# A gated-recurrence layer with two feed-forward layers: wider blocks from the second chunk, the low part of four pairs by TensorE, and other places for the wide operands

## The chip, the cores and the metric

The kernel runs on one core of a Trainium2 chip. The time is the device time of one execution in microseconds (us). Three executions of the kernel before took 1081.52 to 1082.71 us, with a median of 1082.33 us.

## The reference

Two parts follow each other.

```python
# 1. recurrence: B=4 batches, H=8 heads, S=768 steps, D=48
mag = sqrt(a_re**2 + a_im**2); scale = min(mag, 0.999) / (mag + 1e-6)
for t in range(S):
    S_re, S_im = ar*S_re - ai*S_im, ar*S_im + ai*S_re      # state of D x D per head
    S_re += outer(k[t], v[t])
    y[t] = q[t] @ S_re
# 2. two layers over all 3072 tokens x 384, d_ff = 2048
h = x @ w_in;  g = max(h, 0) + alpha * min(h, 0);            x = g @ w_out
h = x @ w_in2; g = h if h >= 1, 0 if h <= -1, else (h+1)**2/4;  out = g @ w_out2
```

The weights come as 64-bit floats. The result has to be close to single precision, so each product of the two layers is made of three matmuls: high part times high part, high times low, low times high.

## The kernel before

**Tokens.** The sequence is cut into 6 chunks of 128 steps. A pair is half a chunk (two batches, 256 tokens); there are 12 pairs, 0 to 11. A pair is made in two slabs of 128 tokens, called p.r (pair 3 has slabs 3.0 and 3.1). VectorE (DVE) makes the products of the gates (`levels`, `fixup`, tile `C`) and multiplies them with q and k (`qkh`, line 265). Twelve DMAs of the queue SP then gather one slab into the tile `st`, of which there is one buffer (lines 269 and 272). TensorE (PE) works on it in `slab_matmul`: scores `sp` (line 286), transposes `kp` (295), outputs `yp` (309) and the state's update `dp` (318). The tokens' high part goes from `yp` to the buffer `xbuf` by ScalarE (ACT, line 312), and the low part, `yp` minus the high part, by DVE (line 313).

**Layers.** `moe` takes a block of tokens through the 16 column groups of a layer. For group f, `h_mm` does 9 matmuls h (line 396), `evac` turns h into a high part `gh` and a low part `gl` with ACT and DVE (lines 409 to 425), and two groups later `y_mm` does 9 matmuls acc (line 436). A block is named by its layer and its first pair (1_2 begins with pair 2) or its number in layer 2 (2_0 to 2_5). Before, blocks 1_0 to 1_3 have one pair, so that a matmul streams 256 columns, and 1_4, 1_6, 1_8 and 1_10 two pairs, 512 columns, as all of layer 2. h1_4.5 is below the h of block 1_4 and group 5, a1_4.5 its acc.

**Weights.** Each of the 16 groups of a layer has one buffer. The raw 64-bit words land there, DVE decodes them (lines 343 to 349), and the high and low part take the same buffer. Weights of layer 2 can take it only after the acc of block 1_10 that reads the old ones. Before, the first four groups (`AHEAD = 4`) use other buffers, `wearly` and `rawearly`, and are decoded before that.

**Order.** A list scheduler sets the order on every engine at build time, by its own estimate of times. On the chip each engine and the queue SP work through their lists in order. Evacuations and the stores of results have priority in it. Which slabs stand in the program ahead of a block is set by `LOOK`: all pairs up to two beyond the block's own.

**Addresses.** In bytes within a partition, modulo 512, the operands of the 512-column matmuls begin here (from the addresses of the built programs; weights and rows within a tile are multiples of 512 apart):

| operand | before | after |
|---|---|---|
| weights `w` of both layers | 480 | 480 |
| weights `wearly`, two tiles | 160 and 256 | none |
| tokens in buffer 0 of `xbuf` (1_4, 1_8, 2_0, 2_2, 2_4) | 32 | 480 |
| tokens in buffer 1 of `xbuf` (1_6, 1_10, 2_1, 2_3, 2_5; after also 1_2) | 480 | 480 |
| `gh` and `gl` | 480 | 224 |

Of the kernel before, what the change touches and what calls it, by code (L numbers as in the profile page):

```python
# [22 lines left out]
GI = 4
NG = T // GI
NU = T // 16
NK = 3
NJ = 2 * NK
NR = 4 * NK
NFC = 16
BLOCKS_A = [1] * 4 + [2] * 4  # L30
HALF_UNTIL, LOOK = 6, 2
VH = 64
VW = H * VH + 32
F64_LEAST = float(np.array(0x38000000, np.uint32).view(np.float32))
F64_MOST = float(np.array(0x47EFFFFF, np.uint32).view(np.float32))
PRIO = 100000
TS = 8
E0, E1, E2, SIDE = 6, 1, 2, 4
AHEAD = 4
PIN = True  # L40
BY_PE = 0
LAG, GB = 2, 3
SCRATCH = 512
RAWS = 11
SHIFT = 8
MI_MOST = 1e4
CAP = 1e10
# [9 lines left out]
def tile_kernel(ctx: ExitStack, tc, ri, qk, v, w1, w2, alpha, seq, vseq, out):  # L57
    nc = tc.nc
    const = ctx.enter_context(tc.tile_pool(name="const", bufs=1))
# [6 lines left out]
    ps_at = ctx.enter_context(tc.tile_pool(name="ps_at", bufs=2, space=PSUM))  # L66
    V, A, G = nc.vector, nc.scalar, nc.gpsimd
# [4 lines left out]
    nident = const.tile([128, 128], F32R, name="nident")  # L72
# [14 lines left out]
        G.memset(t, 0.0)  # L87
        states.append(t)
    chk = const.tile([128, NC, 2, NR], F32, name="chk")
    fac = const.tile([128, NJ, NG + 1], F32, name="fac")  # L90
    def xview(n, wide):

        o = SHIFT if wide == (n == 0) else 0
        return xbuf[n][:, o:o + 2 * NK * 512].rearrange("p (l k n) -> p l k n", l=2, k=NK)

    xbuf, wfirst = {}, const.tile([128, 4, 2 * DM], F32, tag="x1", name="wfirst")
# [14 lines left out]

    x2d = dram.tile([128, NK, NT], F32, name="x2d")
# [102 lines left out]
    def levels(c, js):  # L215
        nj = js.stop - js.start
        C, mie = Cs[c][:, :, js], mis[c][:, js]
        if c == 0:
            V.memset(C[:, 0, :, 0], 1.0)
            V.memset(C[:, 1, :, 0], 0.0)  # L220
        else:
            A.activation(C[:, :, :, 0], Cs[c - 1][:, :, js, NG], AF.Copy)

        def place(i):
            return C[:, :, :, 1 + NG * (GI - 1 - i):1 + NG * (GI - i)]

# [48 lines left out]
    def slab_matmul(p, r, xt, col):  # L275
        c, h2 = divmod(p, 2)
        vt, sn = vts.pop((p, r)), states[2 * h2 + r]

        def slot(h, m):
            return 6 * (h % 2) + 3 * m + h // 2 if h < 6 else 12 + 2 * (h - 6) + m  # L280

        am, kps = [], []
        for f in range(2):
            sp = ps_at.tile([T, 4, T], F32, tag="at", name=f"sp{p}_{r}_{f}")
            for h in range(4):
                nc.tensor.matmul(sp[:, h], st[0:96, slot(4 * f + h, 1)], st[0:96, slot(4 * f + h, 0)], start=True, stop=True)  # L286
            a = p2.tile([T, 4, T], F32, tag="am", name=f"am{p}_{r}_{f}")
            V.tensor_tensor(a, sp, mask.unsqueeze(1).to_broadcast([T, 4, T]), op=ALU.mult)  # L288
            am.append(a)
            yield  # L290
        if c < NC - 1:
            for f in range(2):
                kp = ps_at.tile([T, 4, 96], F32, tag="at", name=f"kp{p}_{r}_{f}")
                for h in range(4):
                    nc.tensor.transpose(kp[:, h], st[0:96, slot(4 * f + h, 1)], ident[0:96, 0:96])
                kt = p2.tile([T, 4, 96], F32, tag="kt", name=f"kt{p}_{r}_{f}")
                A.activation(kt, kp, AF.Copy)
                kps.append(kt)
                yield

        yp = ps_at.tile([128, NK, T], F32, tag="at", name=f"yp{p}_{r}")
        parts = [(j, q, 4 * j + q, 0) for j in range(2) for q in range(4)]
        parts += [(2, q, 2 * q + o, 32) for o in range(2) for q in range(4)]
        sides = [lambda h, w: (sn[:, w:w + 32], st[:, slot(h, 0)])] if c > 0 else []
        sides.append(lambda h, w: (vt[:, w:w + 32], am[h // 4][:, h % 4]))
        for n, side in enumerate(sides):
            for k, (j, q, h, o) in enumerate(parts):
                lhs, rhs = side(h, VH * h + o)
                nc.tensor.matmul(yp[32 * q:32 * q + 32, j], lhs, rhs, start=(n == 0 and k < 4),  # L309
                                 stop=(n + 1 == len(sides) and k >= len(parts) - 4))  # L310
            yield
        A.activation(xt[:, 0, :, col:col + T], yp, AF.Copy)
        V.tensor_tensor(xt[:, 1, :, col:col + T], yp, xt[:, 0, :, col:col + T].bitcast(F32), op=ALU.subtract)
        yield
        if kps:
            dp = ps_at.tile([96, H, VH], F32, tag="at", name=f"dp{p}_{r}")
            for h in range(H):
                nc.tensor.matmul(dp[:, h], kps[h // 4][:, h % 4], vt[:, VH * h:VH * h + VH], start=True, stop=True)  # L318
            dst = sn[0:96].rearrange("p (h d) -> p h d", d=VH)
            if c == 0:  # L320
                A.activation(dst, dp, AF.Copy)
            else:
                V.tensor_tensor(dst, dp, dst, op=ALU.add)
            yield
# [470 lines left out]
def _layout(q, k, v, a_re, a_im, moe_w_in, moe_w_out, moe_alpha, moe2_w_in, moe2_w_out):  # L795
# [12 lines left out]
    vh = vp[..., :H * VH].reshape(NPAIR, 2, T, H, VH)
    vh[..., 0:32] = vs[..., 0:32]
    for o in range(2):  # L810
        vh[..., o::2, 32 + 16 * o:48 + 16 * o] = vs[..., o::2, 32:48]
    vp[..., :H * VH] = vh.reshape(NPAIR, 2, T, H * VH)
# [10 lines left out]
    al = np.ascontiguousarray(moe_alpha.reshape(NFC, 128).T)  # L823
# [29 lines left out]
```

## Time and profile before

| | us |
|---|---|
| median of three executions | 1082.33 |
| the profiled execution, its whole time | 1085.48 |
| its span, first to last instruction | 1083.7 |
| busy in the span: PE, DVE, ACT, POOL | 992.6, 860.7, 464.9, 49.8 |

The profile is of one execution. It lists engines, queues and waits. PE is busy 92% of the span. The clock of PE that the profile shows as granted is 1.00 (2.4 GHz) from 340.4 us to 1081.1 us without a break, and falls to 0.50 (1.2 GHz) in several stretches before. Block 1_1 is on PE from 177 us, 1_2 from 217 us, 1_3 from 274 us, 1_4 from 342 us, 1_6 from 437 us, 1_8 from 527 us, 1_10 from 609 us, and the blocks of layer 2 begin at 674, 741, 807, 874, 940 and 1006 us. In a row of instructions the start is counted from the span's start, "x9" says that nine followed each other, and the last part in brackets is the idle time before them and what ended it.

### The profile page before, as it was taken

To read this page: it belongs to the slowest core of one execution; us is meant where nothing else is said; L and a number is where in the kernel's file an instruction comes from. 1 tells how busy PE (TensorE), PEld (TensorE's weight loads), DVE (VectorE), ACT (ScalarE), POOL (GpSimd) and SP (SyncE) were. 2 spreads that over 40 slices of the span, in tenths; PEclk is the share of its full clock that TensorE was granted. 3 is DMA by queue.
4 is the path that set the end of the run, shared out by engine and by line. 5 is a ranking of instruction groups with operands and counts; after the bars stand their busy time and mean duration, and the time that the engine had idled before them with its cause. 6 is when DMAs were issued, how large, how long until landed. Compare 5 with 4: busy or idle time off the path is not lost.

```text
span 1083.7 us, 16959 instructions
## 1 busy us (share of the span) xinstructions
PE 992.6 (92%) x6401; PEld 837.1 (77%) x6401; DVE 860.7 (79%) x1750; ACT 464.9 (43%) x784; POOL 49.8 (5%) x108
## 2 busy tenths in 40 slices
PE   1369779999987999999999999999999999999997
PEld 0248668989986788888788888788888888888885
DVE  6889979989998999999995769976978855545553
ACT  3347455435633533643433546544444332332332
POOL 2020200000010010000000000000000000000000
PEclk9569888999998999999999999999999999999999
DMA  9570243062215214402332525403415110000000
GB/s 341 177 240 12 64 118 99 12 162 80 67 51 144 86 39 129 122 27 69 87 93 59 175 88 204 147 1 116 151 46 183 58 59 1 1 30 1 30 1 32
DMA packets 66504, 97.52 MB, mean 90 GB/s; under 512 B 8048, under 2 KB 37232, under 8 KB 66416
## 3 DMA queue, kind: packets, MB, share of 16 engines
q1 hardware_dynamic: 66416, 96.38, 28.9%
q8 instruction: 52, 0.85, 0.3%
q14 instruction: 36, 0.29, 0.1%
HBM read 68.03 MB, written 9.44 MB: 71 GB/s over the span
## 4 chain that ended last, share of the span: by engine, by line
PE 68%; DVE 17%; DMA 7%; SPq 3%; issue 2%; ACT 1%; DVEq 0%; ACTq 0%
PE acc L436 31%; PE h L396 30%; PE sp L286 3%; DMA st<-qkh 2%; PE yp L309 2%; SPq L272 2%; DVE t L410 2%; DVE qkh L265 1%; DVE gl L418 1%; DMA C<-in_ri 1%; PE dp L318 1%; DVE C L155 1%; DMA k<-in_qk 1%; DVE C L164 1%; DVE C L163 1%
## 5 line engine op out<-in xcount | busy, mean ns | idle before, releaser
L396 PE MATMUL h<-xbuf,w 128*128 128x512 f32 (+1 forms) x1800 | 395.8, 358 | 3.9 <-DVE t L410 1.3
L436 PE MATMUL acc<-gh,w 128*128 128x512 f32 (+1 forms) x1200 | 357.1, 361 | 3.3 <-ACT o L444 1.7
L396 PEld LDWEIGHTS h<-xbuf,w 128*128 128x128 f32 x1800 | 301.2, 188 | 54.0 <-DVE t L410 1.7
L436 PEld LDWEIGHTS acc<-gh,w 128*128 128x128 f32 x1200 | 217.4, 190 | 37.7 <-ACT o L444 2.4
L436 PE MATMUL acc<-gl,w 128*128 128x512 f32 (+1 forms) x600 | 212.7, 361 | 1.4 <-DVE gl L418 1.3
L422 DVE TENSOR_TENSOR m<-h,t 128x512 f32<-128x512 f32 x96 | 66.0, 689 | 79.7 <-ACT t L420 79.6
L436 PEld LDWEIGHTS acc<-gl,w 128*128 128x128 f32 x600 | 113.9, 190 | 18.6 <-DVE gl L418 2.0
L409 ACT ACTIVATE t<-h,sg 128x256 f32<-128x256 f32 (+1 forms) x128 | 74.0, 579 | 104.6 <-PE h L396 86.5
L424 ACT ACTIVATE gh<-t 128x512 fp32r<-128x512 f32 x96 | 60.5, 630 | 101.1 <-DVE t L423 92.1
L420 ACT ACTIVATE t<-h 128x512 f32<-128x512 f32 x96 | 57.3, 597 | 102.3 <-PE h L396 86.1
L425 DVE TENSOR_TENSOR gl<-t,gh 128x512 fp32r<-128x512 f32 x96 | 66.1, 689 | 43.8 <-ACT gh L424 43.7
L286 PE MATMUL sp<-st 96*128 96x128 f32 x384 | 69.4, 315 | 33.6 <-DMA st<-qkh 31.1
L411 ACT ACTIVATE gh<-t 128x256 fp32r<-128x256 f32 (+1 forms) x128 | 66.7, 522 | 70.9 <-DVE t L410 61.0
L286 PEld LDWEIGHTS sp<-st 96*128 96x128 f32 x384 | 63.1, 222 | 42.3 <-issue 29.7
L410 DVE SCALAR_TENSOR_TENSOR t<-h,sal,t 128x256 f32<-128x256 f32 (+1 forms) x128 | 78.1, 611 | 20.9 <-ACT t L409 20.7
L418 DVE TENSOR_TENSOR gl<-t,gh 128x256 fp32r<-128x256 f32 (+1 forms) x128 | 70.3, 550 | 4.5 <-ACT gh L411 4.4
L423 DVE SCALAR_TENSOR_TENSOR t<-t,m 128x512 f32<-128x512 f32 x96 | 66.1, 689 | 2.2
L379 PE MATMUL wd<-wfirst,ident 128*128 128x384 f32 x64 | 33.1, 620 | 36.0 <-DVE wfirst L349 35.6
L396 PE MATMUL h<-xbuf,wearly 128*128 128x512 f32 x216 | 54.2, 394 | 0.0
L288 DVE TENSOR_TENSOR am<-sp,mask 128x512 f32<-128x512 f32 x48 | 32.9, 684 | 21.4 <-PE sp L286 21.4
L436 PE MATMUL acc<-gh,wearly 128*128 128x512 f32 x144 | 49.1, 394 | 0.0
L396 PEld LDWEIGHTS h<-xbuf,wearly 128*128 128x128 f32 x216 | 40.5, 188 | 9.4 <-issue 0.2
(512 smaller groups left out, 1164.6 us busy)
## 6 DMA issues: line engine op xcount, KB each, us to landing
raw<-in_w SPq DMA_DIRECT2D x56, 384.0 KB, 6.1
st<-qkh SPq DMA_DIRECT2D x96, 144.0 KB, 3.2
rawc<-in_w SPq DMA_DIRECT2D x32, 384.0 KB, 3.5
C<-in_ri SPq DMA_DIRECT2D x10, 768.0 KB, 7.4
v<-in_v SPq DMA_DIRECT2D x24, 272.0 KB, 2.9
k<-in_qk SPq DMA_DIRECT2D x12, 384.0 KB, 5.7
q<-in_qk SPq DMA_DIRECT2D x12, 384.0 KB, 3.2
x2r<-x2d SPq DMA_DIRECT2D x6, 768.0 KB, 4.8
```

The lines of the kernel that those rows point to most:

```text
L286: nc.tensor.matmul(sp[:, h], st[0:96, slot(4 * f + h, 1)], st[0:96, slot(4 * f + h, 0)], start=True, stop=True)
L396: nc.tensor.matmul(hp[:, :n], wt[:, ws], xt[:, kk, :n], start=(k == 0), stop=(k == 8))
L409: A.activation(t, hp, AF.Copy, scale=sg[:, fc:fc + 1])
L410: V.scalar_tensor_tensor(t, hp, sal[:, fc:fc + 1], t, op0=ALU.mult, op1=ALU.max)
L411: A.activation(gh, t, AF.Copy)
L418: V.tensor_tensor(gl, t, gh.bitcast(F32), op=ALU.subtract)
L420: A.activation(t, hp, AF.Relu, scale=0.5, bias=0.5)
L422: V.tensor_tensor(m, hp, t, op=ALU.max)
L423: V.scalar_tensor_tensor(t, t, 1.0, m, op0=ALU.min, op1=ALU.mult)
L424: A.activation(gh, t, AF.Copy)
L425: V.tensor_tensor(gl, t, gh.bitcast(F32), op=ALU.subtract)
L436: nc.tensor.matmul(blk["acc"][m][:, :n], wt[:, ws], gt, start=(fc == 0 and q == 0), stop=(fc == NFC - 1 and q == 2))
```

## The change

1. `BLOCKS_A`: two blocks of one pair (1_0, 1_1), then five of two (1_2, 1_4, 1_6, 1_8, 1_10).
2. `XL_BY_PE = 4`: for pairs 0 to 3 the low part of the tokens is made by a PE matmul that adds minus the high part to `yp`, and an ACT copy, in place of DVE's subtraction.
3. `AHEAD = 0`: no `wearly`; all layer-2 weights are decoded into their own buffers, 14 groups in block 1_10 and two in 2_0.
4. The product with the carry (`tc`) is left out for chunk 0, where the carry is 1.
5. A head's values lie in 48 of 64 places, those of odd heads with the last 16 first; the states' update is 48 wide per head and not 64, and the load of v 512 wide and not 544.
6. Some small tiles are allocated before `xbuf`, and the wide blocks use the other offset (`SHIFT`) of each buffer.

```diff
-BLOCKS_A = [1] * 4 + [2] * 4
+BLOCKS_A = [1] * 2 + [2] * 5
-VW = H * VH + 32
+VW = H * VH
-AHEAD = 4
+AHEAD = 0
+XL_BY_PE = 4
...
+    wchk = const.tile([128, 2, NFC], F32, name="wchk")
+    al = const.tile([128, NFC], F32, name="al")
+    sg = const.tile([128, NFC], F32, name="sg")
     def xview(n, wide):
-        o = SHIFT if wide == (n == 0) else 0
+        o = SHIFT if wide == (n == 1) else 0
...
-        yield from cmul(f"tc{nm}_", C[:, :, :, 4], lambda n: C[:, n:n + 1, :, 0], (nj,))
+        if c:
+            yield from cmul(f"tc{nm}_", C[:, :, :, 4], lambda n: C[:, n:n + 1, :, 0], (nj,))
...
-        parts = [(j, q, 4 * j + q, 0) for j in range(2) for q in range(4)]
-        parts += [(2, q, 2 * q + o, 32) for o in range(2) for q in range(4)]
+        parts = [(j, q, 4 * j + q, q % 2 * 16) for j in range(2) for q in range(4)]
+        parts += [(2, q, 2 * q + o, 32 - 48 * o) for o in range(2) for q in range(4)]
...
-        V.tensor_tensor(xt[:, 1, :, col:col + T], yp, xt[:, 0, :, col:col + T].bitcast(F32), op=ALU.subtract)
+        if p < XL_BY_PE:
+            nc.tensor.matmul(yp, nident, xt[:, 0, :, col:col + T], start=False, stop=True, skip_group_check=True)
+            A.activation(xt[:, 1, :, col:col + T], yp, AF.Copy)
+        else:
+            V.tensor_tensor(xt[:, 1, :, col:col + T], yp, xt[:, 0, :, col:col + T].bitcast(F32), op=ALU.subtract)
...
-            dp = ps_at.tile([96, H, VH], F32, tag="at", name=f"dp{p}_{r}")
+            dp = ps_at.tile([96, H, D], F32, tag="at", name=f"dp{p}_{r}")
-                nc.tensor.matmul(dp[:, h], kps[h // 4][:, h % 4], vt[:, VH * h:VH * h + VH], start=True, stop=True)
+                nc.tensor.matmul(dp[:, h], kps[h // 4][:, h % 4], vt[:, VH * h:VH * h + D], start=True, stop=True)
```

The scheduler makes a new order of it. On PE the scores of slab 3.1 (`sp3_1`) stand before in the middle of block 1_2, whose tokens are then pair 2 alone:

```order
L396 MATMUL h1_2_6_2814<-xbuf1_1346,w1_6_700 128x256 x8
L286 MATMUL sp3_1_0_1844<-st_91 128x128
L286 MATMUL sp3_1_1_1851<-st_91 128x128
L396 MATMUL h1_2_6_2814<-xbuf1_1346,w1_6_700 128x256
L436 MATMUL acc1_2_0_2724<-gh1_2_4_2773,w1_4_602 128x256
```

After, slab 3.1 stands between the last acc of block 1_1 and the first h of block 1_2, which now has both pairs:

```order
L443 MATMUL acc1_1_2_2007<-gh1_1_15_2340,w1_15_1303 128x256
L288 MATMUL sp3_1_0_1841<-st_91 128x128
L288 MATMUL sp3_1_1_1848<-st_91 128x128
L288 MATMUL sp3_1_0_1841<-st_91 128x128 x3
...
L325 MATMUL dp3_1_1906<-v3_1_1821,kt3_1_1_1867 96x48 x4
L317 MATMUL yp3_1_1870<-xbuf1_1340,nident_84 128x384
L403 MATMUL h1_2_0_2937<-xbuf1_1340,w1_0_202 128x512
L403 MATMUL h1_2_1_2963<-xbuf1_1340,w1_1_265 128x512
```

PE has no layer matmul left between block 1_1 and the tokens of slab 3.1. In the queue SP the gather of slab 5.1 stands before behind one of the two loads of chunk 4 (`C4`):

```order
L139 DMA q6_3280<-in_qk 128x768
L129 DMA C4_4084<-in_ri 128x12x128
L269 DMA st_91<-qkh5_1_3264 48x768 x4
L272 DMA st_91<-qkh5_1_3264 32x2x128
L272 DMA st_91<-qkh5_1_3264 16x2x128 x2
```

After, it stands behind both loads and that of `k8`:

```order
L140 DMA q6_2850<-in_qk 128x768
L130 DMA C4_3654<-in_ri 128x12x128 x2
L135 DMA k8_3658<-in_qk 128x768
L271 DMA st_91<-qkh5_1_2834 48x768 x4
L274 DMA st_91<-qkh5_1_2834 32x2x128
```

Two loads, 1.1 MB, have moved ahead of the gather; for slab 3.1 both orders have this form. On DVE the first decode step of layer-2 weights in block 1_10 (`wsecond<-raw2_4`) comes before after the evacuation of group 6:

```order
L418 TENSOR_TENSOR gl1_10_6_6921<-t1_10_6_6919,gh1_10_6_6920 128x512
...
L343 TENSOR_SCALAR wsecond_6269<-wsecond_6269 128x768
...
L345 TENSOR_SCALAR wsecond_6269<-wsecond_6269 128x768
L348 SCALAR_TENSOR_TENSOR wsecond_6269<-raw2_4_6935,wsecond_6269 128x768
```

After, it is that of weight group 0, and it comes after the first evacuation step of group 4:

```order
L417 SCALAR_TENSOR_TENSOR t1_10_4_6413<-h1_10_4_6403,sal_112,t1_10_4_6413 128x512
L350 TENSOR_SCALAR wsecond_6357<-wsecond_6357 128x768
L425 TENSOR_TENSOR gl1_10_4_6415<-t1_10_4_6413,gh1_10_4_6414 128x512
L352 TENSOR_SCALAR wsecond_6357<-wsecond_6357 128x768
L355 SCALAR_TENSOR_TENSOR wsecond_6357<-raw2_0_6354,wsecond_6357 128x768
```

From there to the `gl` of group 2 of block 2_0, DVE has 99 instructions where it had 79 before.

## Rows read from the trace of the kernel before

**Rows 1.** Stages: us; busy of PE, PEld, DVE, ACT, POOL (instructions), PEclk, DMA

```profile
217.00:342.00 125.00, 114.02 (x1231) 109.92 (x1229) 113.27 (x306) 52.69 (x111) 7.40 (x22) 0.95 0.38 101
342.00:609.00 267.00, 261.01 (x2003) 216.50 (x2002) 241.52 (x546) 113.14 (x180) 13.92 (x36) 1.00 0.30 83
609.00:720.00 111.00, 110.09 (x482) 90.02 (x481) 96.51 (x140) 61.99 (x91) 0.00 (x0) 1.00 0.39 133
720.00:1075.00 355.00, 355.00 (x1550) 290.53 (x1549) 220.12 (x316) 129.58 (x205) 0.00 (x0) 1.00 0.15 52
330.20:340.40 10.20, 8.91 (x88) 7.82 (x88) 6.61 (x25) 1.27 (x4) 1.58 (x6) 0.50 0.57 166
```

**Rows 2.** Timeline of PE, slab 5.1: start, length, line, what

```profile
331.33 3.55 PE L286 MATMUL sp<-st 96*128 96x128 f32 x14 [5.41 <-DMA st<-qkh]
...
337.03 1.93 PE L309 MATMUL yp<-st,state 128*32 128x128 f32 x32
...
342.14 0.97 PE L396 MATMUL h<-xbuf,w 128*128 128x512 f32 x3
```

**Rows 3.** Timeline of DVE, the k product of slab 3.1

```profile
226.38 0.95 DVE L265 TENSOR_TENSOR qkh<-C,k 128x768 f32<-128x768 f32 x1
```

**Rows 4.** Timeline of SP's queue, around the gathers of slabs 3.1 and 5.1

```profile
228.98 1.25 SPq L129 DMA_DIRECT2D C<-in_ri  x2
...
313.44 5.13 SPq L272 DMA_DIRECT2D st<-qkh  x8
...
322.58 0.39 SPq L129 DMA_DIRECT2D C<-in_ri  x1
...
326.21 7.54 SPq L272 DMA_DIRECT2D st<-qkh  x8
```

**Rows 5.** Timeline of PE, slab 3.1, then the first h of 1_6 and 1_8

```profile
240.38 0.68 PE L286 MATMUL sp<-st 96*128 96x128 f32 x4 [2.36 <-DVE C L161]
...
251.58 1.08 PE L309 MATMUL yp<-st,state 128*32 128x128 f32 x32
...
436.82 0.94 PE L396 MATMUL h<-xbuf,w 128*128 128x512 f32 x3
...
527.43 0.94 PE L396 MATMUL h<-xbuf,w 128*128 128x512 f32 x3
```

**Rows 6.** The chain of waits: start, length, what (blocks 1_4, 1_10 and 2_2)

```profile
393.21 2.09 PE acc L436 x9
...
635.19 2.04 PE acc L436 x9
...
871.88 2.09 PE acc L436 x9
```

**Rows 7.** DVE by line and shape: count | busy us, mean ns | idle before

```profile
L410 DVE SCALAR_TENSOR_TENSOR t<-h,sal,t 128x512 f32<-128x512 f32 x64 | 47.6, 744 | 17.1 <-ACT t L409 17.0
L418 DVE TENSOR_TENSOR gl<-t,gh 128x512 fp32r<-128x512 f32 x64 | 43.8, 684 | 4.2 <-ACT gh L411 4.2
L410 DVE SCALAR_TENSOR_TENSOR t<-h,sal,t 128x256 f32<-128x256 f32 x64 | 30.4, 477 | 3.8 <-ACT t L409 3.7
L418 DVE TENSOR_TENSOR gl<-t,gh 128x256 fp32r<-128x256 f32 x64 | 26.5, 417 | 0.3 <-ACT gh L411 0.2
L313 DVE TENSOR_TENSOR xbuf<-yp,xbuf 128x384 fp32r<-128x384 f32 x24 | 13.2, 549 | 1.3 <-ACT xbuf L312 1.3
L383 DVE TENSOR_TENSOR w<-wsecond,w 128x768 fp32r<-128x768 f32 x12 | 11.4, 949 | 1.1 <-ACT w L374 1.1
L348 DVE SCALAR_TENSOR_TENSOR wsecond<-raw,wsecond 128x768 int32<-128x768 int32 x12 | 11.4, 948 | 0.0
L343 DVE TENSOR_SCALAR wsecond<-wsecond 128x768 f32<-128x768 f32 x16 | 8.8, 553 | 7.7 <-ACT wsecond L342 7.7
```

**Rows 8.** Timeline of DVE in blocks 1_10 and 2_0

```profile
642.32 0.56 DVE L343 TENSOR_SCALAR wsecond<-wsecond 128x768 f32<-128x768 f32 x1 [1.48 <-ACT wsecond L342]
...
697.89 0.68 DVE L425 TENSOR_TENSOR gl<-t,gh 128x512 fp32r<-128x512 f32 x1
```

**Rows 9.** Timeline of PE, the last acc of a1_10.0 and of a1_10.4

```profile
624.83 0.84 PE L436 MATMUL acc<-gh,w 128*128 128x512 f32 x3
...
636.84 0.39 PE L436 MATMUL acc<-gh,w 128*128 128x512 f32 x1
```

More of the change, by code (lines that the diff above doesn't have):

```diff
@@ L89, in tile_kernel @@
     chk = const.tile([128, NC, 2, NR], F32, name="chk")
-    fac = const.tile([128, NJ, NG + 1], F32, name="fac")
+    wchk = const.tile([128, 2, NFC], F32, name="wchk")
+    al = const.tile([128, NFC], F32, name="al")
+    sg = const.tile([128, NFC], F32, name="sg")
     def xview(n, wide):
-        o = SHIFT if wide == (n == 0) else 0
+        o = SHIFT if wide == (n == 1) else 0
         return xbuf[n][:, o:o + 2 * NK * 512].rearrange("p (l k n) -> p l k n", l=2, k=NK)
@@ L101, in tile_kernel @@
     alloc_x(0)
-    wchk = const.tile([128, 2, NFC], F32, name="wchk")
+    fac = const.tile([128, NJ, NG + 1], F32, name="fac")
     V.memset(fac, ABOVE)
@@ L107, in tile_kernel @@
     V.memset(cap[:, :, 0], 1.0)
-    al = const.tile([128, NFC], F32, name="al")
-    sg = const.tile([128, NFC], F32, name="sg")
     sal = const.tile([128, NFC], F32, name="sal")
@@ L312, in slab_matmul @@
         A.activation(xt[:, 0, :, col:col + T], yp, AF.Copy)
-        V.tensor_tensor(xt[:, 1, :, col:col + T], yp, xt[:, 0, :, col:col + T].bitcast(F32), op=ALU.subtract)
+        if p < XL_BY_PE:
[3 more added lines that the diff above has]
+            V.tensor_tensor(xt[:, 1, :, col:col + T], yp, xt[:, 0, :, col:col + T].bitcast(F32), op=ALU.subtract)
         yield
         if kps:
-            dp = ps_at.tile([96, H, VH], F32, tag="at", name=f"dp{p}_{r}")
+            dp = ps_at.tile([96, H, D], F32, tag="at", name=f"dp{p}_{r}")
             for h in range(H):
-                nc.tensor.matmul(dp[:, h], kps[h // 4][:, h % 4], vt[:, VH * h:VH * h + VH], start=True, stop=True)
-            dst = sn[0:96].rearrange("p (h d) -> p h d", d=VH)
+                nc.tensor.matmul(dp[:, h], kps[h // 4][:, h % 4], vt[:, VH * h:VH * h + D], start=True, stop=True)
+            dst = sn[0:96].rearrange("p (h d) -> p h d", d=VH)[:, :, 0:D]
             if c == 0:
@@ L807, in _layout @@
     vp = np.zeros((NPAIR, 2, T, VW), dtype=v.dtype)
[L808 to L812, printed above, removed]
+    vh = vp.reshape(NPAIR, 2, T, H, VH)
+    vh[..., 0::2, 0:D] = vs[..., 0::2, :]
+    vh[..., 1::2, 0:16], vh[..., 1::2, 16:D] = vs[..., 1::2, 32:], vs[..., 1::2, 0:32]
     def pack_w(wi, wo):
```

## The prediction

> **What bounds the kernel now.** I read the busy time by stages first [rows 1]. From 342 us on PE is nearly always busy: 261.0 of 267 us, 110.1 of 111, 355.0 of 355. There only fewer or quicker matmuls, or a lost wait, change the time. In the last stretch 1550 matmuls take 355.0 us, 229.0 ns each. From 217 to 342 us PE is busy 114.0 of 125 us and DVE 113.3: neither is the bound alone, so I read who waits for whom. The timeline of PE at slab 5.1 shows that it had waited 5.41 us for the gather into `st`, that its matmuls from there ran slowly (the granted clock is 0.50 in that stretch, the lower of the two levels [rows 1]), and that block 1_4 began at 342.14 [rows 2]. I take that moment as the mark of the early part: what comes before it counts by how early it lets 1_4 start.
>
> The timeline of DVE gives the end of the k product of slab 3.1, 226.38 + 0.95 = 227.3 us [rows 3]. In SP's queue two loads of `C` stand between it and the gather [rows 4], and the scores of that slab follow at 240.38 [rows 5]. The starts of 1_6 and 1_8 in the same view give the length of a wide block, 436.82 to 527.43, 90.6 us [rows 5]. Then the chain of waits, which lists matmuls by nines: the same nine take 2.04 us in block 1_10 and 2.09 in 1_4 and 2_2 [rows 6]. The first stand at 480 modulo 512 with all their operands (buffer 1), the others have tokens at 32 (buffer 0). Last, DVE by shapes [rows 7], and the decode of layer-2 weights around 1_10 and 2_0 [rows 8, 9].
>
> **Early part: wide 1_2.** Block 1_2 was pair 2 alone and now holds pairs 2 and 3, so it can't start before slab 3.1 is done. Ahead of that slab's k product DVE loses 6 subtractions of 0.549 us, 3.3, and 4 + 4 evacuation steps of 0.477 and 0.417 us, which belonged to 1_2, 3.6 [rows 7]. The eight steps of `tc`, under 1 us together by my estimate, I leave against the 0.08 us by which one DVE instruction begins before the other ends (227.25 against 227.33 [rows 3]). DVE has little idle time there, so the product ends 7 us earlier, at 220.3. From it to the scores it was 240.38 − 227.33 = 13.05 us; the queue's order around that gather is unchanged, so the scores come at 233.4. PE will then have been without layer work for some ten microseconds, and I expect the lower clock, as at slab 5.1, where scores to first h took 342.14 − 331.33 = 10.8 us and `yp` 1.93 us against 1.08 at full clock [rows 2, 5]. First h of 1_2: 233.4 + 10.8 = 244.2.
>
> Its length: 288 matmuls, 32 nines at 2.04 us, are 65.3 us. 1_6 took 90.6, with four slabs in it: (90.6 − 65.3)/4 = 6.3 us a slab. 1_2 holds three (4.0, 4.1, 5.0): 65.3 + 19.0 = 84.3. It ends at 328.5. Slab 5.1 comes next. Its gather is now queued behind both loads of `C` and one of k, where one `C` load was behind it [rows 4]. These loads wait for nothing late: the gather of slab 5.0 is gone from the queue by 319, and I take the new one as landed before 328.5, since DVE has 6.9 us less to do. So PE goes on at the higher clock: 9 to 10.8 us, the lower end being the 10.8 less the 0.85 us of `yp` and about as much for the rest. Then 1_4 begins at 337.5 to 339.3, against 342.14: −2.8 to −4.6, **−4 taken**. The bounds are far apart. If the scores are as early as the product allows and the clock stays up, 1_2 starts at 238 and 1_4 at 331.3, −11; if the gather is late by what DVE gives back, it is +9 (worked out with the rivals). The value taken stands nearest to the measured steps, 13.05 and 10.8.
>
> `XL_BY_PE` exchanges 8 subtractions of 0.549 us for 8 matmuls of 384 columns and 8 copies by ACT. Seven of the eight chains lie in PE's idle time or beside 1_1. At slab 3.1 the chain is `yp`, copy, matmul, copy in place of `yp`, copy, subtraction: 0 to +0.6 us. It is inside the bounds above. Values 48 wide: 0 for PE, in whose slabs weight loads are as many as before; 0 for DMA. The wide evacuation of pairs 2 and 3 saves DVE 16 × (2 × (0.477 + 0.417) − 0.744 − 0.684) = 5.8 us [rows 7], hidden behind PE inside 1_2.
>
> **Middle, 342 to 609 us.** 1_4 and 1_8 took their tokens from buffer 0. If they go from 2.09 to 2.04 us a nine, PE loses 2 × 32 × 0.05 = 3.2 us of work. But the tokens of the next pairs come from DVE, busy 241.5 of 267 us here [rows 1], and its work up to block 1_8 falls by only 3.6 us, most of it already spent in the early part. **−1 taken**, bounds −3 and +1.
>
> **`AHEAD = 0`.** Before, the first decode step of 1_10 came at 642.32 [rows 8], 5.1 us after the last acc of group 4, 636.84 + 0.39 [rows 9]. Now group 0's buffer is the first; its acc ends at 625.7 [rows 9], so decode can begin about 12 us earlier. From there to the `gl` of group 2 in 2_0 (697.89 + 0.68 [rows 8]) DVE has 20 instructions more: 6 × 0.553 + 6 × 0.948 + 2 × 0.949 + 3 × 0.744 + 3 × 0.684 = 15.2 us [rows 7], 13.6 after the overlap of 0.08 each. In the 55.6 us before, DVE was nearly full (96.5 of 111 in the stage [rows 1]). So that `gl` comes 1.6 us later against the same PE time, and the two groups decoded in 2_0 add some more until group 9, where PE's own 28.6 us give room. PE waits where it did not: **+2 taken**, bounds 0 and +5.
>
> **Last part, 720 to 1075 us.** All operands but `gh` and `gl` now stand at 480, these at 224. If 224 counts as the same place as 480 (they differ by 256), all nines are at 2.04, that is 226.7 ns a matmul: 1550 × 0.2267 = 351.4, **−3.6**. If not, at the 230.5 ns of mixed rates (half way from 226.7 to over 232), 357.3, +2.3; at 2.09, 232.2 ns, +4.9. No row shows an operand pair 256 apart. I choose the first: of 32 and 480 the trace shows two places 64 apart in the circle of 512 that cost something, and 160 and 256 of `wearly` are no multiples of 256 from 480 either.
>
> The Trainium skill, "SBUF — State Buffer", section "SBUF: two separate sides", says that only the port pair shared by GpSimd and VectorE causes contention on the engine side, and that PE never waits on anyone. By that rule the place of an operand would change nothing and this term, with the middle's, would be 0. The trace disagrees so far: the same nine take 2.04 or 2.09 by block [rows 6].
>
> **Sum.** −4 − 1 + 2 − 3.6 = −6.6 us. The profiled execution took 1085.48 (span 1083.7 and 1.8 around it), so its like would take 1078.9. It lies 3.15 us above the median of 1082.33; against that the forecast is 1075.7, **1076**.
>
> **Rivals.**
> A. 224 is another place than 480. The tail then costs +2.3 to +4.9 and the middle about +1: −4 + 1 + 2 + 3.5 = +2.5, 1085. For it: nothing shows a period of 256. Against: it would need that 224, not 32 alone, disturbs.
> B. Block 1_2 waits longer than 1_2 of one pair was worth. Place: PE between 1_1 and 1_2. If DVE's 7 us are not given to the k product but to other work, and the gather waits for its turn, 1_2 begins at 256 (251.58 + 1.08 [rows 5], yp's time before, and 3 us for copies and the low part). It ends at 340.3, 1_4 begins at 350, +8; with −1 + 2 − 3.6 that is +5.4, 1088. The point from which it decides: a start of 1_2 beyond 248 makes the early part a loss, beyond 251 the whole. For it: the list of DVE has products of later chunks too, and the gather shares the queue with loads; against: DVE's order puts that product early.
> C. Slab 3.1 comes at full clock, 1_2 at 238, 1_4 at 331.3, −11: 1082.3 − 11 − 1 + 2 − 3.6 = 1069. Against: the 5.41 us wait before was enough for the lower clock [rows 2].
> D. The place of operands counts for nothing, what differs between blocks is something else: −4 + 2 = −2, 1080. Against: 2.04 and 2.09 go with the buffer in all three blocks [rows 6].
>
> **How the numbers follow.** Forecast 0.42, A 0.20, B 0.19, C 0.12, D 0.07. About 0.2%, 2.2 us, is what a measurement of this kernel can tell from no change. Faster by more: nearly all of the forecast (0.41), C (0.12), half of D: 0.57. Within: half of A, half of D, a little of B and of the forecast: 0.16. Slower: half of A and most of B, 0.27. The likeliest case's own range is 1071 to 1081. With C below and A and the near part of B above it is 1067 to 1087; the far part of B, a start of 1_2 after 256, and C with all bounds at their ends are left out.
>
> **What would show it.** Right: first h of 1_2 near 244 us and of 1_4 near 338; nines of 2.04 us in 2_0, 2_2 and 2_4; the last stretch at 227 ns a matmul; in 2_0 an idle time of PE of about 2 us behind `gh` or `gl`. A shows as 2.07 to 2.09 in all acc nines, also those of buffer 1. B shows as a first h of 1_2 later than 248, with an idle PE that waits for `st` and a clock of 0.5 behind it. C shows as 1_2 before 240 at a clock of 1.0. The forecast is wrong as a whole if 1_4 begins later than 345 us, or if PE's idle time in 2_0 is over 6 us.

## The result and the profile after

| | before | after |
|---|---|---|
| median of five executions, us | 1082.71 | 1074.46 |
| lowest and highest | 1081.52, 1085.35 | 1073.14, 1077.15 |
| the profiled execution, whole time | 1085.48 | 1073.14 |
| first h of 1_4, of 1_10, of 2_0, of 2_1 | 342.1, 608.7, 673.8, 741.6 | 337.1, 599.8, 663.8, 733.5 |

The ratio after to before is 0.9912, 95% interval [0.9894, 0.9929]: 8.2 us less between the medians, where 6.3 had been forecast. The two profiled executions lie 12.3 us apart, because that of before is 2.8 us above its median and that of after 1.3 below; the steps below are read from them, and their sum is that of the pair.

The stages after, in the columns of [rows 1], cut at the first h of 1_4, 1_10, 2_0 and 2_1:

```profile
217.00:337.10 120.10, 111.24 (x931) 94.78 (x930) 106.66 (x264) 48.45 (x80) 5.67 (x22) 0.94 0.37 99
337.10:599.80 262.70, 260.33 (x1998) 216.66 (x1999) 230.11 (x528) 107.95 (x172) 12.16 (x36) 1.00 0.28 76
599.80:663.80 64.00, 64.00 (x284) 52.97 (x283) 50.92 (x74) 36.19 (x53) 0.00 (x0) 1.00 0.51 175
663.80:733.50 69.70, 67.57 (x295) 54.92 (x294) 62.52 (x92) 36.90 (x54) 0.00 (x0) 1.00 0.22 77
733.50:1063.90 330.40, 330.40 (x1459) 273.54 (x1458) 208.76 (x299) 122.48 (x196) 0.00 (x0) 1.00 0.16 55
```

The same stretches of before, which the rows above cut elsewhere:

```profile
342.10:608.70 266.60, 260.61 (x2000) 216.28 (x2000) 241.12 (x545) 112.75 (x179) 13.92 (x36) 1.00 0.30 83
608.70:673.80 65.10, 65.10 (x289) 53.88 (x288) 51.88 (x74) 36.80 (x53) 0.00 (x0) 1.00 0.45 152
673.80:741.60 67.80, 66.89 (x290) 53.94 (x289) 56.28 (x83) 32.78 (x50) 0.00 (x0) 1.00 0.21 74
741.60:1075.80 334.20, 334.20 (x1460) 273.59 (x1458) 208.77 (x299) 122.70 (x196) 0.00 (x0) 1.00 0.16 55
```

So up to 1_4 the kernel is 5.0 us ahead; from there to 1_10 it wins 3.9, PE's idle time falling from 6.0 to 2.4 us; 1_10 gives 1.1 and 2_0 costs 1.9; the five blocks from 2_1 on give 3.8. That is 11.9 us. The window of 1_10 holds five matmuls fewer than before and that of 2_0 five more, so these two are read together: they cost 0.8, of which PE's idle time, 2.1 us instead of 0.9, is 1.2, and quicker matmuls give back 0.4.

Each of these starts is read from one trace. The kernel `a_xcurve` (below) does the same work in the same order as the kernel after up to block 2_0, and in its trace 1_4 and 1_10 begin about 4 us later:

```profile
341.04 0.97 PE L404 MATMUL h<-xbuf,w 128*128 128x512 f32 x3 [2.03 <-ACT xbuf L316]
...
604.12 1.07 PE L404 MATMUL h<-xbuf,w 128*128 128x512 f32 x4
```

So a difference of under 4 us between two traces at such a mark shows nothing by itself. The length from 1_4 to 1_10 is steadier, 263.1 us there and 262.7 here.

The DVE timeline, the k product of slab 3.1, which ended at 227.3 before [rows 3]:

```profile
215.69 0.95 DVE L267 TENSOR_TENSOR qkh<-C,k 128x768 f32<-128x768 f32 x1
```

SP's queue behind it [rows 4]; the two loads of `C` and that of k go first, and the gather is issued from 221.46:

```profile
216.79 1.09 SPq L130 DMA_DIRECT2D C<-in_ri  x2
217.93 3.44 SPq L135 DMA_DIRECT2D k<-in_qk  x1
221.46 2.98 SPq L271 DMA_DIRECT2D st<-qkh  x4
```

PE's timeline from there [rows 2, 5], the first h of 1_2 and of 1_4 among it:

```profile
228.88 1.99 PE L288 MATMUL sp<-st 96*128 96x128 f32 x12 [3.59 <-DMA st<-qkh]
...
234.93 1.94 PE L312 MATMUL yp<-st,state 128*32 128x128 f32 x32 [0.73 <-ACT kt L299]
...
241.55 7.50 PE L403 MATMUL h<-xbuf,w 128*128 128x512 f32 x27
...
337.13 0.96 PE L403 MATMUL h<-xbuf,w 128*128 128x512 f32 x3 [2.03 <-ACT xbuf L315]
```

The wait, the `yp` of 1.94 us (the lower clock) and the start of 1_2 are as forecast in kind. In 2_0 PE waits for evacuations and for the copies of the results (DVE's side of that stretch before is in [rows 8]):

```profile
681.88 0.50 PE L443 MATMUL acc<-gh,w 128*128 128x512 f32 x1 [1.32 <-ACT o L451]
...
686.14 4.37 PE L403 MATMUL h<-xbuf,w 128*128 128x512 f32 x18 [0.79 <-DVE m L429]
```

And the chain of waits in block 2_2, whose nines took up to 2.09 us before [rows 6]:

```profile
800.99 2.04 PE acc L443 x9
803.03 2.04 PE h L403 x9
```

### The profile page after: what moved, and what is told of

The parts are those of the page before. It is cut to its first block, busy times and chain, and to the rows that moved or that the text cites. A ratio compares the mean times of both kernels' runs of the same rounds, so it can differ in the third digit from the quotient of the medians.

```text
span 1071.4 us, 16278 instructions
## 1 busy us (share of the span) xinstructions
PE 985.0 (92%) x6121; PEld 823.9 (77%) x6121; DVE 851.7 (79%) x1702; ACT 460.7 (43%) x757; POOL 55.2 (5%) x108
## 4 chain that ended last, share of the span: by engine, by line
PE 72%; DVE 15%; DMA 5%; SPq 5%; issue 2%; ACT 1%; DVEq 0%; ACTq 0%
PE h L403 32%; PE acc L443 31%; DMA st<-qkh 3%; PE yp L312 3%; PE sp L288 3%; SPq L274 2%; DVE qkh L267 2%; PE dp L325 1%; SPq L271 1%; DVE t L417 1%; DVE C L156 1%; PE wd L386 1%; DVE C L165 1%; DVE C L164 1%; DVE gl L425 1%
## 5 line engine op out<-in xcount | busy, mean ns | idle before, releaser
L403 PE MATMUL h<-xbuf,w 128*128 128x512 f32 (+1 forms) x1872 | 446.1, 378 | 5.9 <-ACT xbuf L318 2.2
L443 PE MATMUL acc<-gh,w 128*128 128x512 f32 (+1 forms) x1248 | 394.6, 376 | 1.3 <-ACT o L451 1.3
L403 PEld LDWEIGHTS h<-xbuf,w 128*128 128x128 f32 x1872 | 335.6, 191 | 67.9 <-ACT xbuf L318 2.5
L443 PE MATMUL acc<-gl,w 128*128 128x512 f32 (+1 forms) x624 | 233.1, 377 | 1.6 <-DVE gl L425 1.6
L416 ACT ACTIVATE t<-h,sg 128x512 f32<-128x512 f32 (+1 forms) x112 | 69.9, 625 | 115.2 <-PE h L403 102.1
L418 ACT ACTIVATE gh<-t 128x512 fp32r<-128x512 f32 (+1 forms) x112 | 63.6, 568 | 81.1 <-DVE t L417 75.9
L427 ACT ACTIVATE t<-h 128x512 f32<-128x512 f32 x96 | 57.1, 596 | 94.5 <-PE h L403 78.4
L417 DVE SCALAR_TENSOR_TENSOR t<-h,sal,t 128x512 f32<-128x512 f32 (+1 forms) x112 | 74.8, 667 | 25.7 <-ACT t L416 25.2
L425 DVE TENSOR_TENSOR gl<-t,gh 128x512 fp32r<-128x512 f32 (+1 forms) x112 | 68.0, 607 | 8.7 <-ACT gh L418 8.7
L156 DVE TENSOR_TENSOR C<-C 128x384 f32<-128x384 f32 (+3 forms) x106 | 39.8, 375 | 1.7
L325 PEld LDWEIGHTS dp<-v,kt 128*96 128x96 f32 x320 | 31.5, 176 | 5.0 <-issue 3.7
```

The source lines that it names most:

```text
L403: nc.tensor.matmul(hp[:, :n], wt[:, ws], xt[:, kk, :n], start=(k == 0), stop=(k == 8))
L416: A.activation(t, hp, AF.Copy, scale=sg[:, fc:fc + 1])
L417: V.scalar_tensor_tensor(t, hp, sal[:, fc:fc + 1], t, op0=ALU.mult, op1=ALU.max)
L418: A.activation(gh, t, AF.Copy)
L425: V.tensor_tensor(gl, t, gh.bitcast(F32), op=ALU.subtract)
L427: A.activation(t, hp, AF.Relu, scale=0.5, bias=0.5)
```

## The experiments

All ratios are to the kernel before, timed beside it on the same chip; that of the kernel after is 0.9912 [0.9894, 0.9929]. Where two kernels with a ratio each are compared, the bounds are from the ends of both intervals. Where a kernel has a single time, only its trace is read, since single times of one kernel lay up to 8.5 us apart.

### The places of the operands

**Only the places, on the kernel before** (`b_offset`). The small tiles of item 6 go ahead of `xbuf`, and:

```diff
-        o = SHIFT if wide == (n == 0) else 0
+        o = SHIFT if wide == (n == 1) else 0
```

> The kernel before with only the places changed: small tiles allocated ahead of the token buffers and the other SHIFT, so that the tokens of all wide blocks begin at 480 modulo 512, as w, gh and gl already do (wearly stays at 160 and 256). Theory (the place of the tokens sets the spacing of matmuls): blocks 2_0, 2_2 and 2_4 go from 230 to 231.5 ns a matmul to about 228.3, as 2_1, 2_3 and 2_5 have; 3 x 288 x 2.5 ns = 2.2 us in layer 2, and up to 1.4 us in 1_4 and 1_8: 2 to 3.5 us less, ratio 0.997 to 0.998. Rival D (the place counts for nothing): the blocks keep their two rates, ratio 1.000.

Measured: ratio 0.9975 [0.9960, 0.9990], 2.7 us less. Blocks 2_1 and 2_2, of which the second had 66.5 us before (807.3 to 873.8):

```profile
738.40:804.10 65.70, 65.70 (x290) 54.04 (x289) 53.28 (x74) 28.46 (x45) 0.00 (x0) 1.00 0.35 120
804.10:869.80 65.70, 65.70 (x289) 54.04 (x288) 51.56 (x76) 27.90 (x44) 0.00 (x0) 1.00 0.32 108
```

Rival D is out: nothing but addresses moved, and the programs of both kernels hold the same instructions in the same order on every engine. The 0.4 us that are left to 65.3 are the four groups in `wearly`.

**Tokens at five places** (`a_xcurve`):

```diff
+        o = o if at is None else at
...
-        xt = xview(bi % 2, True)
+        xt = xview(bi % 2, True, (0, 0, 8, 8, 4, 4)[bi])
```

> The kernel after, with the tokens of the six blocks of layer 2 at 480, 448, 0, 480, 496 and 464 modulo 512 (weights stay at 480, gh and gl at 224). Theory: 2_0 and 2_3 keep 226.7 ns a matmul, the other four go to 229 to 232, and the time is 3 to 6 us longer. Rival D: 226.7 ns in all six. If only a distance of 64 counts (32 against 480 in the kernel before), 448, 0, 496 and 464 stay at 226.7 too.

Measured: 2_0 and 2_3 are quick, the others not. The windows are blocks 2_1 (tokens at 448), 2_2 (at 0), 2_3 (at 480) and 2_4 (at 496):

```profile
738.40:804.90 66.50, 66.50 (x289) 54.04 (x288) 53.31 (x74) 28.46 (x45) 0.00 (x0) 1.00 0.36 119
804.90:871.70 66.80, 66.80 (x290) 54.07 (x289) 51.65 (x76) 28.12 (x44) 0.00 (x0) 1.00 0.31 107
871.70:937.00 65.30, 65.30 (x290) 54.07 (x289) 34.66 (x50) 22.52 (x37) 0.00 (x0) 1.00 0.08 25
937.00:1003.60 66.60, 66.60 (x289) 53.94 (x288) 34.66 (x50) 21.30 (x36) 0.00 (x0) 1.00 0.03 13
```

Even 16 bytes cost 1.3 us a block of 288 matmuls. In 2_1 the chain shows that the nines of h pay, and that nines of acc, whose operands did not move, can stay at 2.04:

```profile
738.52 2.10 PE h L404 x9
740.63 2.04 PE acc L444 x9
```

Later in 2_1 ten acc take 2.31 us, 231 ns each, so some of them pay too. In 2_5 (tokens at 464) h is at 2.10 and acc at 2.04. At 0 and 496 the acc nines take up to 2.08; why acc pays in some blocks and not in 2_5 stays open.

**gh and gl at 352 instead of 224** (`a_gh352`):

```diff
+        if not pads:
+            pads.append(p2.tile([128, 32], F32, tag="pad", name="pad", bufs=1))
+            V.memset(pads[0], 0.0)
         gh = p2.tile([128, 512], F32R, tag="gh", name=f"gh{nm}", bufs=GB)[:, o:o + n]
```

> The kernel after, with a pad of 128 bytes ahead of gh and gl, so that they begin at 352 instead of 224 modulo 512; tokens and weights stay at 480. Theory (224 counts as the same place as 480, since they are 256 apart, and 352 does not): the nines of acc go from 2.04 us to 2.07 or more, and those of h perhaps with them; 1 to 4 us longer. Rival (only the tokens' place counts, or places 128 apart are the same too): all stay at 226.7 ns a matmul.

Measured: 1_10 and every block from 2_1 on are slower, the acc nines most; block 2_1 took 66.5 us. The lines are of 2_2:

```profile
806.55 2.09 PE acc L446 x9
808.65 2.07 PE h L403 x9
```

So gh's place does count: 352, 128 bytes from 224 and from 480, costs time, and 224, 256 bytes from 480, does not. The kernel with `a_vh64` (below) has gh and gl at 480 and shows the same 226.7 ns.

**Everything 128 bytes further** (`a_all128`), a pad of 128 bytes ahead of tokens, weights, gh and gl:

```diff
+    pad = const.tile([128, 32], F32, name="pad")
+    V.memset(pad, 0.0)
```

> The kernel after with a pad of 128 bytes ahead of tokens, weights, gh and gl alike: tokens and weights at 96, gh and gl at 352 modulo 512. With gh and gl alone at 352 the matmuls took 229.6 (h) and 232.2 ns (acc). Theory a (the distance of the operands to one another decides): 226.7 ns everywhere. Theory b (the place itself decides, 224 modulo 256): 229 to 232 ns everywhere, 3 to 8 us longer.

Measured, blocks 2_1 and 2_2:

```profile
736.50:801.80 65.30, 65.30 (x289) 54.07 (x288) 53.29 (x74) 28.68 (x45) 0.00 (x0) 1.00 0.35 121
801.80:867.10 65.30, 65.30 (x290) 54.07 (x289) 51.68 (x76) 28.07 (x44) 0.00 (x0) 1.00 0.31 109
```

Theory a, as far as two places (480 and 96) show it: the distance of the operands to one another decides, not the place.

### The blocks, the low part, the carry

**Only the new blocks, on the kernel before** (`b_blocks2`):

```diff
-BLOCKS_A = [1] * 4 + [2] * 4
+BLOCKS_A = [1] * 2 + [2] * 5
```

> The kernel before with only BLOCKS_A changed to two blocks of one pair and five of two. Theory (DVE's work ahead of slab 3.1 sets the start of 1_2): without XL_BY_PE and with the first carry product DVE has about 4 us more before the product of slab 3.1 than in the kernel after, so 1_2 begins at 245 to 246 and 1_4 at 340.5 to 342; the time is within 2 us of the kernel before, and within 1 us if the places in buffer 0 eat what is won. Rival (the blocks alone are the early gain): 1_4 begins at 337, as in the kernel after, 5 us less. Rival B of the prediction, here without DVE's relief: 1_2 later than 250, the kernel slower by 4 us or more.

Measured: ratio 0.9984 [0.9969, 0.9998]. The product of slab 3.1 ends only 0.9 us earlier than before; PE waits 8.44 us and 1_2 begins at 249.8, 1_4 at 345.8.

```profile
238.30 3.33 PE L286 MATMUL sp<-st 96*128 96x128 f32 x14 [8.44 <-DMA st<-qkh]
...
249.79 0.97 PE L396 MATMUL h<-xbuf,w 128*128 128x512 f32 x3 [0.63 <-ACT xbuf L312]
```

That is rival B's mechanism, with 1_4 3.7 us late, which one pair of traces does not show for certain. Yet 1_10 begins at 608.8, as before. DVE's last k product ends at 580.5 in both: its work up to there is 2.0 us less (524.3 against 526.3) and its idle time 2.1 us more. So a later 1_4 did not carry through to 1_10, and the time is even 0.16% less.

**The old blocks, on the kernel after** (`a_blocks4`): the same edit the other way.

> The kernel after with the old BLOCKS_A, four blocks of one pair and four of two. Prediction's step (the wide 1_2 wins about 4 us by 1_4, with the relief of DVE in it): 1_4 begins at 340 or later, 3 us or more slower. Rival, from the kernel before with the new blocks alone (1_4 at 345.8 instead of 342.1, the time less by 0.16%): the blocks are worth nothing by themselves; 1_4 begins at 331 to 337 and the time stays within 2 us of the kernel after.

Measured: ratio 0.9900 [0.9883, 0.9917], against the kernel after 0.9988 [0.9954, 1.0023]. 1_4 begins at 327.9, 9.2 us earlier, and 5.3 of them are gone by 1_10 (595.9). The rival holds, and by more than it said (331 to 337): the wide 1_2 wins nothing by 1_4, it costs, and the time stays the same within what can be told.

```profile
219.00:327.90 108.90, 105.71 (x1203) 102.41 (x1203) 101.84 (x283) 51.79 (x111) 6.90 (x22) 1.00 0.38 103
327.90:595.90 268.00, 262.79 (x2002) 218.90 (x2001) 234.42 (x537) 109.85 (x176) 14.06 (x36) 0.99 0.28 75
```

**The low part by DVE again** (`a_xl0`):

```diff
-XL_BY_PE = 4
+XL_BY_PE = 0
```

> The kernel after with XL_BY_PE = 0: DVE subtracts for the low part of all pairs again. Theory (DVE's work ahead of the product of slab 3.1 sets the start of 1_2): 6 subtractions of 0.55 us come back ahead of it, so from the first h of 1_1 to the first h of 1_2 it takes 66 us instead of 62.8, and 1_4 begins 3 us later; about half of it comes back by 600 us, as DVE has less left to do then: 1 to 3 us slower than the kernel after. Rival (the edit is neutral, its chains lie in PE's idle time): 62.8 us and the same time. Second rival (the low part by PE costs a longer chain at slab 3.1): 1_2 starts earlier than in the kernel after.

Measured: ratio 0.9849 [0.9829, 0.9869], against the kernel after 0.9936 [0.9899, 0.9975]: about 7 us **less**, a miss of all three expectations. The product of slab 3.1 ends at 217.4, 0.8 us later than after, 1_2 begins at 241.3 as after, 1_4 at 334.7 and 1_10 at 593.4. The 3.3 us that the theory expected do appear from the first h of 1_1 (176.1) to that of 1_2: 65.2 us, against 61.8 after (the 62.8 of the expectation was counted from an h of 1_0). But 1_1 itself begins 3.7 us earlier. From 1_4 to 1_10, and then DVE's side up to the last k product (the second and third line are of `a_xl0` and of the kernel after):

```profile
334.70:593.40 258.70, 258.00 (x2002) 216.10 (x2001) 229.26 (x527) 107.94 (x172) 15.94 (x36) 1.00 0.28 79
0.00:563.60 563.60, 484.05 (x3831) 411.99 (x3832) 520.80 (x1231) 253.16 (x433) 57.65 (x108) 0.95 0.37 106
0.00:566.20 566.20, 489.05 (x3823) 415.30 (x3824) 517.04 (x1221) 253.27 (x439) 55.19 (x108) 0.92 0.36 105
```

That is 258.7 us with 0.7 idle, against 262.7 with 2.4. DVE has 3.8 us more work up to the last k product (520.8 against 517.0) and 6.4 us less idle time (42.8 against 49.2; 50.5 and 52.9 in `a_all128` and `a_xcurve`, which have the order of the kernel after). So `XL_BY_PE = 4` takes work from DVE and adds more idle time than that. Why is argued and not shown: subtractions that may have filled its waits are gone, PE and ACT, which DVE waits for, have more to do, and the order is another.

**The first carry product kept** (`a_tc`):

```diff
-        if c:
+        if True:
             yield from cmul(f"tc{nm}_", C[:, :, :, 4], lambda n: C[:, n:n + 1, :, 0], (nj,))
```

> The kernel after with the first carry product kept (tc for chunk 0 too, 8 small steps of DVE). The prediction put it under 1 us. With it the scheduler lists 203 rows on DVE ahead of the k product of slab 1.0 instead of 189 (before: 215), 432 ahead of that of slab 3.1 instead of 419. Theory a (only the steps count): the product of slab 1.0 ends by 108 us, that of 3.1 by 218, the time grows by at most 1 us. Theory b (leaving it out lets the scheduler put decode steps and evacuations behind the slab): the product of slab 1.0 ends at 111 to 115 instead of 106.6, that of 3.1 at 219 to 222, and the time is 2 to 5 us longer.

Measured: ratio 0.9933 [0.9917, 0.9950], against the kernel after 1.0021 [0.9988, 1.0057]: 2 us by the medians, within what can be told. Theory b holds for the order of things, and at slab 3.1 by more than expected; its 2 to 5 us are not shown. The products of slabs 1.0 and 3.1, which end at 106.6 and 216.6 in the kernel after:

```profile
109.69 0.94 DVE L267 TENSOR_TENSOR qkh<-C,k 128x768 f32<-128x768 f32 x1
...
225.12 0.95 DVE L267 TENSOR_TENSOR qkh<-C,k 128x768 f32<-128x768 f32 x1
```

1_2 begins at 250.0, 8.4 us later than in the kernel after, and 1_4 at 340.2, but 1_10 at 599.0, no later than there.

**The values 64 wide again** (`a_vh64`; the lines of item 5 as before the change):

```diff
-VW = H * VH
+VW = H * VH + 32
...
-            dp = ps_at.tile([96, H, D], F32, tag="at", name=f"dp{p}_{r}")
+            dp = ps_at.tile([96, H, VH], F32, tag="at", name=f"dp{p}_{r}")
```

> The kernel after with the values in their old form: 64 wide, v of 544 columns, the states' update 64 wide (gh and gl then stand at 480 instead of 224). The prediction put this edit at nothing: first h of 1_1 to first h of 1_2 in 62 to 64 us, 226.7 ns a matmul in layer 2, and the time that of the kernel after. Rival: the blocks alone brought the product of slab 3.1 only 0.9 us forward, the whole change 10.7; if the wide update is what holds the product, it takes 66 us or more.

Measured: one time, 1073.72 us; the product of slab 3.1 at 215.6, and 226.7 ns a matmul in layer 2, as expected. From the first h of 1_1 (184.9) to that of 1_2 (242.0) it takes 57.1 us, below the 62 to 64 expected, since 1_1 begins 5.1 us later. 1_4 begins at 333.3, 3.8 us earlier, and 1_10 at 600.5, 0.6 later: once more the two do not go together.

**Early weights again** (`a_ahead4`):

```diff
-AHEAD = 0
+AHEAD = 4
```

> The kernel after with AHEAD = 4: four groups of layer-2 weights are decoded early again, into wearly, which here stands at other places than the weights. Theory (two terms that cancel): 2_0 loses the 1.2 us of idle PE that AHEAD = 0 added and takes about 67 us instead of 69.7, while the four groups with other places bring all blocks of layer 2 from 226.7 to about 228.3 ns a matmul, 6 x 288 x 1.6 ns = 2.8 us, and DVE has some 15 us more to do in block 1_8, which costs 0 to 2 us before 1_10: 0 to 3 us slower than the kernel after. Rival (the prediction's +2 for AHEAD = 0 with no other effect): 2 us faster.

Measured: ratio 0.9912 [0.9893, 0.9930], that of the kernel after to four digits. The windows are 1_10, 2_0 and 2_1 (the bound between the first two may be 2 us off):

```profile
598.90:665.50 66.60, 66.60 (x295) 55.16 (x294) 52.70 (x76) 37.93 (x54) 0.00 (x0) 1.00 0.41 138
665.50:732.10 66.60, 66.27 (x290) 53.91 (x288) 56.07 (x82) 32.61 (x50) 0.00 (x0) 1.00 0.21 76
732.10:797.80 65.70, 65.70 (x289) 54.08 (x288) 53.37 (x74) 28.47 (x45) 0.00 (x0) 1.00 0.35 120
```

From 1_10 to 2_1 it takes 133.2 us, 0.5 less than after (64.0 + 69.7), and 1_10 begins 0.9 earlier; against that each of the five later blocks takes 0.4 more, 2.0 together. The terms cancel within what can be told, as the theory said.

### The queue, and a version that beats both

**Loads behind the gather** (`a_gather`):

```diff
         if nxt > c and u > 1:
-            load_chunk(nxt)
-        if after and u > 1:
+            with tc.issue_after(stacked[2 * c - 1, 1]):
+                load_chunk(nxt)
+                load_k(after[0])
+        elif after and u > 1:
             load_k(after[0])
```

> The kernel after, with the loads of a chunk and of its first k issued behind the gather of the slab that frees their buffers, instead of ahead of it. In the kernel after, the k product of slab 3.1 ends at 216.6 and its gather is issued from 221.5, behind two loads of C and one of k. Theory (the queue's order is a term of the 12 us from the product to the scores): the gather is issued from about 217.5, the scores come about 4 us earlier, with less idle PE ahead of them the clock may stay at 1.00, and 1_2 begins 4 to 8 us earlier, against 62.8 us after 1_1; half or more of it stays in the end: 2 to 6 us less than the kernel after. Rival (the transfers share the bandwidth anyway, so the loads only move): the gather lands as late, no gain. Second rival (chunk 3's levels then start later and DVE falls behind): 1_2 earlier, 1_4 not, no gain or a loss.

Measured: ratio 0.9846 [0.9824, 0.9867], against the kernel after 0.9933 [0.9894, 0.9973]. The gather is issued from 219.55 and the loads follow at 228.50. The scores begin at 223.61, 5.3 us earlier, 1_2 at 236.3, 1_4 at 328.4. The clock fell all the same (`yp` 1.94 us). Most of it is given back in 1_4, where PE waits for a slab: from 1_4 to 1_6 it takes 99.2 us instead of 92.1, and 1_10 begins at 597.5, 2.3 us earlier than after. How the other runs come to 7 us less by the medians this one trace, of one of its slower executions (1071.49 us, median 1069.58), does not show.

```profile
230.82 1.94 PE L312 MATMUL yp<-st,state 128*32 128x128 f32 x32 [0.73 <-POOL cw L251]
...
236.30 4.01 PE L403 MATMUL h<-xbuf,w 128*128 128x512 f32 x16
...
334.00 0.76 PE L288 MATMUL sp<-st 96*128 96x128 f32 x2 [4.68 <-DMA st<-qkh]
```

**Both edits that gained** (`a_best`): `XL_BY_PE = 0` and the loads behind the gather.

> The kernel after with both edits that gained: XL_BY_PE = 0, and the loads of a chunk behind the gather that frees their buffers. If the gains add: 1_2 begins at 235 to 237, 1_10 at 589 to 593, ratio 0.978 to 0.982. If they are one gain found twice (DVE and the tokens of the later pairs set the time by 600 us): the ratio of either alone, 0.984 to 0.986.

Measured: ratio 0.9823 [0.9805, 0.9841], median 1064.35 against 1084.35 us: the quickest of all, and 0.9910 [0.9875, 0.9946] of the kernel after. Against `a_xl0` alone it is 0.9974 [0.9935, 1.0012], so that the gains add only in part, if at all. 1_2 begins at 238.5, 1_4 at 332.5, 1_10 at 591.4.

## Why the prediction was right

The time and its sign came out, 1076 forecast and 1074.46 measured, but in part by luck: the steps did so in unequal measure, and errors of both signs met.

1. **The chain to 1_2**: right in kind. Product at 216.6 (220.3 said), 12.2 us to the scores (13.05), 12.7 to the first h (10.8), start at 241.6 (244.2). From there to 1_4 95.6 us (93.3 to 95.1). The 5.0 us won by 1_4 are the 4 forecast, as far as single traces tell: with the two orders 1_4 begins at 342.1 and 340.8 (before, `b_offset`), and at 337.1, 337.4, 337.9 and 341.0 (after, `a_ahead4`, `a_all128`, `a_xcurve`). In SP's queue the prediction counted two loads of `C` ahead of the gather; a load of k stands there too, before and after (3.2 and 3.4 us in the queue), and moving all of them behind the gather brings the scores 5.3 us forward (`a_gather`).
2. **That the wide 1_2 wins them, and that 1_4 is the mark**: wrong. With the old blocks 1_4 begins 9 us earlier (`a_blocks4`), and the new blocks alone win nothing by there (`b_blocks2`). Nor does the early part count by how early it lets 1_4 start: against the kernel each was made from, 1_4 moves by +3.7, −9.2, −3.8 and −2.4 us and 1_10 by +0.1, −4.0, +0.6 and −6.5 (`b_blocks2`, `a_blocks4`, `a_vh64`, `a_xl0`). What brings the product of slab 3.1 forward is the order on DVE, by `a_tc`: with the carry product kept it ends at 226.1, nearly the 227.3 of before. Ahead of the product of slab 1.0 stand 215 rows before and 189 after; it ends at 118.7 and 106.6. Built but not run: the kernel before with `tc` left out has 194 there, and the kernel after with `tc` and `XL_BY_PE = 0` again 215. So leaving out the carry product of chunk 0, priced under 1 us by its eight steps, lets the scheduler move other rows, of weights and evacuations, behind the slab: 13 of them on the kernel before, 6 in the kernel after (203 rows in `a_tc`). What it is worth in time without `XL_BY_PE` was not run.
3. **`XL_BY_PE` at 0 to +0.6**: the largest miss. It costs about 7 us of what the rest wins. The prediction priced its one chain at slab 3.1 and not the idle time that DVE has with it (49.2 us against 42.8).
4. **The middle, −1**: −3.9 in the pair, of which the places alone give 1.2 (265.4 us from 1_4 to 1_10 in `b_offset`). The reason given, that DVE limits it, fits (its idle and PE's idle fall together in `a_xl0`), but the term was too small, since the 3.6 us of relief are too few. DVE's work up to the last k product fell by 9.3 us, from 526.3 in the kernel before to 517.0:

```profile
0.00:580.50 580.50, 497.84 (x4128) 433.06 (x4129) 526.33 (x1272) 260.38 (x469) 49.79 (x108) 0.93 0.36 105
```

   The prediction does not show where its 3.6 comes from; its own 8 subtractions (4.4) and wide evacuation (5.8) come to 10.2. The values 48 wide, put at 0, take another 2.1 from DVE: 16 updates of the state at 546 ns instead of 680. None of it is early decode of layer 2, which begins at 594.4 in the kernel before; put back (`a_ahead4`), it does not delay 1_10 (598.9).
5. **`AHEAD = 0`, +2**: 1_10 and 2_0 together cost 0.8, with 1.2 us more idle time of PE in 2_0, inside the bounds of 0 and +5. What was not priced is that the same edit removes `wearly` with its other places, and those cost 0.4 us in each later block. Net 0 within what can be told (`a_ahead4`).
6. **The last part, −3.6**: −3.8 in the five blocks. 224 counts as 480, as chosen. Rival A's doubt was sound: with gh at 352 the acc nines take 2.09 (`a_gh352`). Rival D, which the Trainium skill's rule ("SBUF — State Buffer", section "SBUF: two separate sides", PE never waits on anyone) would give, is refuted by `b_offset`: 2.7 us, ratio 0.9975 [0.9960, 0.9990], from addresses alone.

The errors were these: too much for the blocks and nothing for the waits that come with `XL_BY_PE`, against too little for the order and the middle. The single edits do not add up to the whole: +7 for `XL_BY_PE`, −2 for `tc` (not clear of noise), about 0 for blocks, values and `AHEAD` and −3 for places make +2, where the whole is −8. So of the causes the places alone are shown, with 2.7 us; some 10 us belong to no single edit, and where they come from stays open. Each edit lets the scheduler make another order on all engines, and leaving out `tc` and `XL_BY_PE = 4` may stand in for each other in part: only with both undone does the built order have the 215 rows of before again, and that kernel was not run. How much of the 7 us is the new order and how much PE's and ACT's work itself stays open too.

## What to carry to other kernels

Price an edit in a scheduled kernel by the order that comes out, not by its instructions: eight small steps moved 6 to 13 others, and an edit that relieved the busier engine lost time, as its idle time grew by more than its work fell. Do not take the start of one block as the measure of all that comes before it: here it moved by up to 9 us, and the start of a later block did not move with it. Try each part of such a change by undoing it: here one part cost nearly as much as the whole won. And look at the addresses when equal matmuls run at two rates: here the cure moved addresses and nothing else.

## What the runs showed of the hardware

Matmuls of 512 columns follow each other in 226.7 ns when tokens, weights and gh stand at the same place modulo 512, and gh 256 bytes away counts as the same (480, 480 and 480 or 224; 96, 96 and 352). They take up to 2.10 us for nine, 233 ns each, when tokens stand 16, 32 or 64 bytes off, and up to 2.09 when gh stands 128 bytes off. The matmuls of the operand that is off pay most, but those between can pay too (2.08 for nine with tokens at 0 and 496, 2.04 at 464). And a slab at the lower clock came even where PE had waited for no more than 0.7 us at a time (`a_gather`: the granted clock was 0.89 from 225 to 229 us, when PE was busy 2.73 of 4.0 us, and 0.57 from 229 to 236; from 229 to 230 it was 0.50, the lower of the two levels).
